# Transposing x tiles in pairs by column half, moving three small loads to GpSimd's queue, and dropping two filler products, at the head of a gated attention/MLP kernel

## The chip, the cores and the metric

The kernel runs on one core of one Trainium2 chip. The metric is device time in microseconds (us) of one execution.

The engines are TensorE (PE in the profile; PEld is its weight load), VectorE (DVE), ScalarE (ACT), GpSimd (POOL) and SyncE (SP). SPq, ACTq and POOLq in the profile are those engines issuing data transfers. "L592" is line 592 of the kernel in question; the changed kernel's lines are numbered 9 lower from the transposes on, because its text is shorter.

## The reference, cut to what matters

```
x: [1, 2048, 512] bf16
g   = sigmoid((x * gate_w).sum(-1))
qkv = x @ wqkv                        # 32 heads of 16, as [3, heads, S, 16]
o   = for each position: softmax over 8 keys at distance 0, 2, ..., 14, times their values
a   = o @ wo
h   = layernorm(x)
b   = token-mixing MLP over S: gelu(h^T @ w1 + b1) @ w2 + b2, transposed back
out = g * a + (1 - g) * b
```

Q, K and V come from x with its 512 columns on the partitions, so x has to be transposed. The first 512 rows (four tiles, x0 to x3) are transposed by TensorE. The other 1536 rows are transposed by three DMA transposes that SyncE issues.

## The kernel before: the parts that matter

The kernel builds a list of operations with their dependences. A list scheduler with estimated durations then fixes each engine's order before anything runs. TensorE's order is the order of the source, except for two operations (`sum0`, `sum1`).

```python
# loads; "sp" is SyncE's queue, "act" is ScalarE's
for k_ in (0, 2):
    xq(k_, "sp");  xq(k_ + 1, "act")      # x tiles, 128 KB each
    wqq(k_, "sp"); wqq(k_ + 1, "act")     # rows of wq, 128 KB each
load("gw", ...); load("b1", ...); load("b2", ...)     # 1, 3.5 and 4 KB, on SyncE
load("wk", ...)                                        # 512 KB
ld_w("wv", 2, 0, 4, "wv")                              # 512 KB
for k_ in range(1, 4):
    ld_x(4 * k_, 4)                                    # four x tiles
    ld_xt(k_)                                          # DMA transpose of 512 rows of x

# head of TensorE's program
pe_tx(0)                  # four 128x128 transposes of tile 0, into two banks
pe_tx(1)
PE(f_fill(2), ...)        # two products of ones, results unused
pe_q0(0, 0)               # Q of rows 0-255,   wq row block 0: 4 products of 256 columns
pe_tx(2)
pe_tx(3)
pe_q0(0, 1)
PE(f_tb, ...)             # b1, gate_w, b2 turned onto partitions
pe_q0(1, 0); pe_q0(1, 1)  # Q of rows 256-511, wq row blocks 0 and 1
pe_q0(2, 2); pe_q0(2, 3)  # all 512 rows, wq row blocks 2 and 3
# ... then K of rows 0-511 (first operation that needs wk), V, and the rest

# of each transposed tile, VectorE copies columns 0-255 and ScalarE columns 256-511
def xt_ev(t):
    for k_, eng in enumerate(("dve", "act")):
        ...

# VectorE: layernorm statistics of each x tile; attention products of 128x4096 each.
# After the second of these products GpSimd issues a transfer of 1 MB, SBUF to SBUF,
# that adds one buffer to another:
def qaddd(x_, y_, s_, h=h):
    o_, i_ = (sub(PB[b_], s_ * 4096, [(1, 4096)]) for b_ in (x_, y_))
    qkd[h, s_] = sch.dma("pool", lambda e: e.dma_start(o_, i_, accum_op=ALU.add, ...), ...,
                         reads=[PS[y_][s_]], writes=[PS[x_][s_]], ...)
```

Of the kernel before, what the change touches and what calls it, by code (L numbers as in the profile page):

```python
# [5 lines left out]
BF16 = mybir.dt.bfloat16  # L6
# [3 lines left out]
AF = mybir.ActivationFunctionType  # L10
AX = mybir.AxisListType

S = 2048
# [5 lines left out]
NST = S // 128  # L19
NFT = F // 128  # L20
# [260 lines left out]
class _Mem:  # L281
# [17 lines left out]
    def view(self, name, dtype, dims, extra=0, p0=0, np_=128):  # L299
        base = self.arena[:].bitcast(dtype)  # L300
        pst = base.ap[0][0]
        esz = mybir.dt.size(dtype)
        o = self.off[name]
        assert o % esz == 0
        return bass.AP(base.tensor, p0 * pst + o // esz + extra, [[pst, np_]] + [list(d) for d in dims])


def bass_gated_mix__sliding_local_dilated__mixer_token_mlp__prompt_kernel(nc, A_x, A_wqkv, A_wo, B_x, B_w1, B_b1, B_w2, B_b2, gate_w, out, dbg=None):
    with contextlib.ExitStack() as es:
# [37 lines left out]
        ps = es.enter_context(nc.psum_tensor("ps", [128, 8, 512], FP32))  # L347
        esem = {e: es.enter_context(nc.semaphore("sem_" + e)) for e in ("pool", "act", "dve", "pe")}
        sch = _Sched()
        A = sch.add  # L350
# [8 lines left out]
        X = view("X", BF16, [(D, NST), (1, D)])  # L359
        XT = view("XT", BF16, [(S, 4), (1, S)])  # L360
# [39 lines left out]
        IDENT = view("IDENT", BF16, [(1, 128)])  # L400
        ONES = view("ONES", BF16, [(1, 128)])
        RP = view("RP", BF16, [(1, 32)])
        GWREP = view("GWREP", BF16, [(32, 4), (1, 32)])
        MASK = view("MASK", BF16, [(PAD, NW), (1, PAD)], np_=32)
        B1R = view("ROWS", BF16, [(1, 128)], np_=NFT)
        B2R = view("ROWS", BF16, [(1, 128)], extra=128, np_=NST)
        GWR = view("ROWS", BF16, [(1, 128)], extra=256, np_=4)
        so = [0]

        def small(n, dims=None, extra=0):  # L410
            v_ = view("SMALL", FP32, dims or [(1, n)], extra=so[0] + extra)
            so[0] += n
            return v_
# [17 lines left out]
        B1C = small(NFT)  # L431
        B2C = small(NST)
# [5 lines left out]
        def psb(bank):  # L438
            return ps[:, bank, :].bitcast(BF16)

        def sub(ap_, offs, dims):
            return bass.AP(ap_.tensor, ap_.offset + offs, [list(ap_.ap[0])] + [list(d) for d in dims])
# [8 lines left out]
        def act(o_, i_, f_, **kw):  # L451
            return lambda e: e.activation(out=o_, in_=i_, func=f_, **kw)  # L452
# [32 lines left out]
        def load(name, dst, src, nbytes, writes, transpose=False, queue="sp", issue=0.5, order=True, deps=(), after=()):  # L485
            ds = sch.dsem(name)

            def fn(e):
                if transpose:
                    return e.dma_start_transpose(dst, src)  # L490
                return e.dma_start(dst, src)  # L491
            op = sch.dma(queue, fn, nbytes, ds, issue=issue, writes=writes, deps=list(deps) + late_dep[0],
                         after=list(after) + ([last_ld[queue]] if order and queue in last_ld else []), name=name)
            if order:
                last_ld[queue] = op
            return op
# [4 lines left out]
        def ld_w(name, tn, d0, d1, res):  # L501
            load(name, WQKV[:, d0:d1, tn * D:(tn + 1) * D], wqkv_v[:, d0:d1, tn * D:(tn + 1) * D], (d1 - d0) * 128 * D * 2, [res])
# [14 lines left out]
        for k_ in (0, 2):  # L517
# [1 line left out]
            xq(k_ + 1, "act")  # L519
            wqq(k_, "sp")  # L520
            wqq(k_ + 1, "act")
        load("gw", GWR, gate_w.rearrange("(t p) -> t p", p=128), 1024, ["gwr"], issue=0.4)
        load("b1", B1R, B_b1.rearrange("(t p) -> t p", p=128), 4096, ["b1r"], issue=0.4)
        load("b2", B2R, B_b2.rearrange("(t p) -> t p", p=128), 4096, ["b2r"], issue=0.4)
        load("wk", WQKV[:, 0:4, D:2 * D], wqkv_v[:, 0:4, D:2 * D], 4 * 128 * D * 2, ["wk"])
        ld_w("wv", 2, 0, 4, "wv")
        for k_ in range(1, 4):
            ld_x(4 * k_, 4)
# [12 lines left out]
        C1 = nc.const_aps.tensor(1.0, (128, 128), BF16)  # L541
# [9 lines left out]
        def PE(fn, dur, reads, writes, name, prio=0):  # L551
            op = A("pe", fn, dur, reads=reads, writes=writes, after=([chain[0]] if chain[0] is not None else []), name=name, prio=prio)
            chain[0] = op
            return op

        PE(f_warm, 2.6, [], ["b7"], "warm")

        def f_fill(n):
            def fn(e):
                ins = None  # L560
                for _ in range(n):
                    ins = e.matmul(ps[:, 0, 0:256], lhsT=C1, rhs=nc.const_aps.tensor(1.0, (128, 256), BF16), start=True, stop=True)
                return ins
            return fn

        def f_tx(t):
            def fn(e):
                ins = None
                for dt in range(4):
                    o_ = (dt % 2) * 128  # L570
                    ins = e.transpose(out=psb(4 + 2 * (t % 2) + dt // 2)[:, o_:o_ + 128],  # L571
                                      in_=X[:, t, dt * 128:(dt + 1) * 128], identity=IDENT)
                return ins
            return fn

        extl = {}

        def xt_ev(t):
            for k_, eng in enumerate(("dve", "act")):
                bk = 4 + 2 * (t % 2) + k_  # L580
                src = sub(psb(bk), 0, [(128, 2), (1, 128)])
                dst = sub(XT, 2 * k_ * S + t * 128, [(S, 2), (1, 128)])
                extl[eng] = A(eng, (lambda s_, d_: lambda e: e.tensor_copy(out=d_, in_=s_))(src, dst) if eng == "dve" else act(dst, src, AF.Copy),  # L583
                  0.27 if eng == "dve" else 0.35, reads=["b%d" % bk], writes=["xt0_%d_%d" % (t, k_)], name="ext%d_%d" % (t, k_), prio=-30)

        def f_q0(hb, dt):
            c0, c1 = ((0, 256), (256, 512), (0, 512))[hb]
# [7 lines left out]
            return fn  # L595

        def pe_tx(t):
            PE(f_tx(t), 0.35, ["x%d" % t, "ident"], ["b%d" % (4 + 2 * (t % 2)), "b%d" % (5 + 2 * (t % 2))], "tx%d" % t)
            xt_ev(t)

        def pe_q0(hb, dt):
            PE(f_q0(hb, dt), 0.87 if hb == 2 else 0.44, ["xt0_%d_%d" % (t_, dt // 2) for t_ in ((0, 1), (2, 3), (0, 1, 2, 3))[hb]] + ["wq%d" % dt], ["b%d" % dl for dl in range(4)],
               "q0_%d_%d" % (hb, dt))

        def f_tb(e):
            e.transpose(out=psb(4)[:, 512:512 + NFT], in_=B1R, identity=IDENT[0:NFT, 0:NFT])  # L606
            e.transpose(out=psb(4)[:, 576:580], in_=GWR, identity=IDENT[0:4, 0:4])  # L607
            return e.transpose(out=psb(4)[:, 544:544 + NST], in_=B2R, identity=IDENT[0:NST, 0:NST])  # L608

        pe_tx(0)  # L610
        pe_tx(1)
        PE(f_fill(2), 0.4, [], ["b0"], "fill1")
        pe_q0(0, 0)
        pe_tx(2)
        pe_tx(3)
        pe_q0(0, 1)
        PE(f_tb, 0.17, ["b1r", "b2r", "gwr", "ident"], ["b4"], "t_b12")
        A("dve", lambda e: e.tensor_copy(out=GWREP, in_=sub(psb(4), 576, [(1, 4), (0, 32)])), 0.2, reads=["b4"], writes=["gwrep"], name="gwrep", prio=-20)
        A("dve", lambda e: e.tensor_copy(out=B1C, in_=psb(4)[:, 512:512 + NFT]), 0.15, reads=["b4"], writes=["b1c"], name="b1c", prio=-20)
        A("dve", lambda e: e.tensor_copy(out=B2C, in_=psb(4)[:, 544:544 + NST]), 0.15, reads=["b4"], writes=["b2c"], name="b2c", prio=-20)  # L620
        pe_q0(1, 0)
        pe_q0(1, 1)
        pe_q0(2, 2)
        pe_q0(2, 3)
        XT0 = ["xt0_%d_%d" % (t, k_) for t in range(4) for k_ in range(2)]

# [48 lines left out]
        for dl in range(4):  # L675
# [3 lines left out]
          reads=["k%d_1" % dl for dl in range(4)], writes=["khalo"], name="khalo")  # L679
# [10 lines left out]
        for t in range(NST):  # L690
            A("dve", (lambda t_: lambda e: e.bn_stats(out=ST6[:, t_, :], in_=X[:, t_, :]))(t), 0.67,  # L691
              reads=["x%d" % t], writes=["st%d" % t], name="st%d" % t, prio=-20, after=[extl["dve"]])
# [6 lines left out]
          reads=["md"], writes=["vv"], name="ln_var", prio=-20)  # L699
# [3 lines left out]
          reads=["ms", "rstd"], writes=["nmr"], name="ln_nmr", prio=-20)  # L703
        for t in range(NST):
            A("dve", (lambda t_: lambda e: e.tensor_scalar(out=X[:, t_, :], in0=X[:, t_, :], scalar1=col(RSTD, t_), scalar2=col(NMR, t_),  # L705
                                                           op0=ALU.mult, op1=ALU.add))(t), 0.33,
              reads=["rstd", "nmr", "st%d" % t], writes=["x%d" % t], name="ln%d" % t, prio=-10)
# [22 lines left out]
        for h in range(2):  # L730
# [27 lines left out]
            for s_ in range(2):  # L758
                qadd(bb[0], bb[2], s_)
            b0 = bb[0]  # L760
            A("pe", f_sum(h, b0, h == 0), 1.2 + (1.0 if h == 0 else 0), reads=PS[b0] + ["rp"] + ((XTALL + ["gwrep"]) if h == 0 else []),
              writes=LGB + (["b3"] if h == 0 else []), name="sum%d" % h, prio=-100, delay=0.2)
# [4 lines left out]
            if h == 0:  # L767
                A("dve", tt(psub(LOG[0], 0, 32, 0, [(UT_, NW), (1, PAD)]), psub(LOG[0], 0, 32, 0, [(UT_, NW), (1, PAD)]), MASK, ALU.add), 0.2,
                  reads=["mask"], writes=["log0"], name="msk", prio=-30)
# [16 lines left out]
            for c in range(4):  # L786
                src = psub(ATT[h], 32 * c, 32, 0, [(0, 4), (1, NW * UT_)])
                dst = sub(AVW[h], c * NW * UT_, [(1, NW * UT_)])
                prev = sch.dma("pool", (lambda d_, s_: lambda e: e.dma_start(d_, s_))(dst, src), 524288, sch.dsem("av%d_%d" % (h, c)), issue=1.0,  # L789
                               reads=["att%d" % h], writes=["avw%d_%d" % (h, c)] + al, after=[prev] if prev else [], name="av%d_%d" % (h, c))  # L790
# [11 lines left out]
          reads=["ebt"], writes=["e1"], name="e1", prio=-20)  # L802
# [60 lines left out]
        for ft in range(NFT):  # L863
            bank = MLPB[ft]
            for half in range(2):
# [3 lines left out]
              reads=["b%d" % bank, "b1c"], writes=["ut%d" % ft] + (["wq0", "wq1", "wq2", "wq3", "wk", "wv"] if ft == 0 else []), name="gel%d" % ft, table=GELU)  # L869
# [56 lines left out]
        for hf, (c0, c1) in enumerate(CH):  # L926
            bank = lastb[hf]
            PE(f_wo(L, bank, c0, c1), 0.44, ["ot%d" % (L // 2), "wo"], ["b%d" % bank], "wo%d_%d" % (L, hf))
            if hf == 0:
                A("act", act(OUTS[:, 4, c0:c1], ps[:, bank, 0:c1 - c0], AF.Identity, scale=col(OMG, L), bias=col(C2, L)), 0.55,  # L930
                  reads=["b%d" % bank, "omg", "c2"], writes=["outs4"], name="ev%da" % L)
            else:
                A("dve", (lambda bank_, a_, b_: lambda e: e.tensor_scalar(out=OUTS[:, 4, a_:b_], in0=ps[:, bank_, 0:b_ - a_], scalar1=col(OMG, L),  # L933
                                                                          scalar2=col(C2, L), op0=ALU.mult, op1=ALU.add))(bank, c0, c1), 0.35,
                  reads=["b%d" % bank, "omg", "c2"], writes=["outs4h"], name="ev%db" % L)
# [82 lines left out]
```

## Time and profile before

Before: 165.93 us (median of 3; 165.66 to 166.41). The profiled execution took 165.79 us.

| what | value |
|---|---|
| span of the profiled execution | 164.1 us |
| TensorE / VectorE busy | 97% / 92% |
| first x transpose on TensorE | 3.73 us |
| first Q product / first K product | 5.12 / 9.73 us |
| wk issued / landed | 3.85 / 9.60 us |
| x2, x3, wq2 landed | 5.19, 5.38, 5.94 us |

The page's part 1 (busy time, share of the span, number of instructions) and the first line of its part 4 (share of the chain that ended last, by engine), kernel before:

```profile
PE 159.4 (97%) x792; PEld 77.0 (47%) x808; DVE 150.7 (92%) x126; ACT 75.4 (46%) x104; POOL 11.9 (7%) x35
...
PE 93%; DMA 2%; SPq 1%; ACT 1%; issue 1%
```

TensorE bounds the kernel: almost all of the chain is TensorE work. The timeline of TensorE in the head of the kernel before (start us, length us, engine, line, operation, shapes, count, and in brackets idle time and what ended it):

```profile
3.73 1.01 PE L571 MATMUL ps<-arena 128*128 128x128 bf16 x8 [0.16 <-DMA arena<-in_A_x_dram]
4.53 0.57 PE L562 MATMUL ps<-const-bfloat16-1.0 128*128 128x256 bf16 x2
5.12 0.63 PE L592 MATMUL ps<-arena 128*128 128x256 bf16 x4
5.59 0.61 PE L571 MATMUL ps<-arena 128*128 128x128 bf16 x8
6.04 0.60 PE L592 MATMUL ps<-arena 128*128 128x256 bf16 x4
6.78 0.16 PE L606 MATMUL ps<-arena 14*128 14x14 bf16 x1
...
6.92 2.79 PE L592 MATMUL ps<-arena 128*128 128x256 bf16 x15
9.73 1.46 PE L659 MATMUL ps<-arena 128*128 128x512 bf16 x6
```

Eight transposes, two fillers, four Q products, eight transposes, four Q products, the bias transposes, the rest of Q, and K from 9.73 us. From there TensorE never waits, so the time of this kernel is the start of K plus a constant.

The timeline of VectorE, kernel before:

```profile
11.43 2.29 DVE L449 TENSOR_TENSOR arena<-arena 128x4096 bf16<-128x4096 bf16 x1 [0.39 <-ACT arena L452]
13.64 2.46 DVE L691 BATCH_NORM_STATS2 arena<-arena 128x6 f32<-128x512 bf16 x4
16.67 2.47 DVE L691 BATCH_NORM_STATS2 arena<-arena 128x6 f32<-128x512 bf16 x4 [0.56 <-DMA arena<-in_A_x_dram]
19.06 2.27 DVE L449 TENSOR_TENSOR arena<-arena 128x4096 bf16<-128x4096 bf16 x1
```

The second 128x4096 product runs at 19.06 us, behind the statistics of x8 to x11. GpSimd's accumulating transfer is issued after it, as the timeline of GpSimd shows:

```profile
21.64 1.32 POOL L746 DMA_DIRECT2D arena<-arena  x1 [19.56 <-DVE arena L449]
```

### The profile page before, as it was taken

Reading aid. Unit: us, or ns where it says so; the run is one execution under the profiler, and the core shown is the slowest. Engines: PE = TensorE matmul, PEld = TensorE weight load, DVE = VectorE, ACT = ScalarE, POOL = GpSimd, SP = SyncE. Lnnn points to the kernel's source line nnn. Section 1 sums busy time; section 2 is a strip of 40 time slices with the busy share of each in tenths; the row PEclk is TensorE's granted clock in tenths of the full one; section 3 lists DMA queues with packets and bytes.
Section 4 is the critical chain, followed back from the end, with each engine's and each line's share of the span. In section 5 each row is a group of like instructions: output and inputs, shape, how many; then the busy total and the mean of one; then the engine's idle time right before and its main releaser. Section 6 shows DMA issues by size and latency. Waiting matters only on the chain.

```text
span 164.1 us, 1991 instructions
## 1 busy us (share of the span) xinstructions
PE 159.4 (97%) x792; PEld 77.0 (47%) x808; DVE 150.7 (92%) x126; ACT 75.4 (46%) x104; POOL 11.9 (7%) x35
## 2 busy tenths in 40 slices
PE   7999999999999999999999999999999999999993
PEld 3745555555544444444444344444444444444641
DVE  0679999999999999999999999999999999999950
ACT  3356677666773699953211669210121111111164
POOL 3000030020000000005000000005000222000000
PEclk9999999999999999999999999999999999999999
DMA  4999999919499287999998994993996899981014
GB/s 153 284 240 249 258 178 252 185 22 188 92 310 290 50 230 202 291 290 259 158 205 245 278 250 145 295 242 113 280 226 177 164 205 184 211 201 36 32 57 135
DMA packets 44668, 32.24 MB, mean 197 GB/s; under 512 B 7924, under 2 KB 42228, under 8 KB 44660
## 3 DMA queue, kind: packets, MB, share of 16 engines
q1 hardware_dynamic: 41428, 22.06, 51.8%
q0 software_dynamic: 2512, 9.44, 28.9%
q10 hardware_dynamic: 720, 0.62, 1.1%
q8 instruction: 6, 0.10, 0.2%
q14 instruction: 2, 0.02, 0.0%
HBM read 18.88 MB, written 2.10 MB: 128 GB/s over the span
## 4 chain that ended last, share of the span: by engine, by line
PE 93%; DMA 2%; SPq 1%; ACT 1%; issue 1%
PE ps L857 29%; PE ps L884 29%; PE ps L659 23%; PE ps L893 8%; DMA arena<-in_B_b_dram 2%; PE ps L592 2%; SPq L491 1%; PE ps L721 1%; ACT arena L452 1%; PE ps L716 1%; PE ps L606 0%; PE ps L608 0%; PE ps L607 0%
## 5 line engine op out<-in xcount | busy, mean ns | idle before, releaser
L449 DVE TENSOR_TENSOR arena<-arena 128x4096 bf16<-128x4096 bf16 (+8 forms) x79 | 131.9, 1718 | 1.3 <-ACT arena L452 0.4
L884 PE MATMUL ps<-arena 128*128 128x512 bf16 (+2 forms) x234 | 50.0, 366 | 0.2
L857 PE MATMUL ps<-arena 128*128 128x512 bf16 x218 | 48.5, 379 | 0.3
L452 ACT ACTIVATE arena<-ps,arena 128x512 bf16<-128x512 f32 (+1 forms) x30 | 21.8, 732 | 58.0 <-PE ps L893 40.5
L452 ACT ACTIVATE arena<-ps 128x512 bf16<-128x512 f32 (+3 forms) x53 | 33.1, 629 | 18.4 <-PE ps L659 10.9
L659 PE MATMUL ps<-arena 128*128 128x512 bf16 x173 | 38.0, 379 | 0.2
L884 PEld LDWEIGHTS ps<-arena 128*128 128x128 bf16 x238 | 22.8, 98 | 25.9
L857 PEld LDWEIGHTS ps<-arena 128*128 128x128 bf16 x224 | 21.7, 98 | 26.9 <-ACT arena L452 0.7
L659 PEld LDWEIGHTS ps<-arena 128*128 128x128 bf16 x176 | 19.8, 113 | 18.3 <-DVE arena L691 0.5
L893 PE MATMUL ps<-arena 128*128 128x512 bf16 (+2 forms) x66 | 15.5, 366 | 0.1
L953 ACT ACT_TABLE_LOAD x11 | 14.1, 1283 | 2.9 <-issue 2.7
L691 DVE BATCH_NORM_STATS2 arena<-arena 128x6 f32<-128x512 bf16 x16 | 10.0, 679 | 0.7 <-DMA arena<-in_A_x_dram 0.6
L452 ACT ACTIVATE arena<-arena 128x16 f32<-128x16 f32 (+5 forms) x10 | 6.8, 679 | 7.3 <-DVE arena L449 7.0
L893 PEld LDWEIGHTS ps<-arena 128*128 128x128 bf16 x68 | 6.5, 98 | 7.3
L789 POOL DMA_DIRECT2D arena<-arena x8 | 4.3, 561 | 73.9 <-DVE arena L449 73.9
L705 DVE TENSOR_SCALAR arena<-arena 128x512 bf16<-128x512 bf16 x16 | 5.3, 402 | 0.0
L826 POOL DMA_DIRECT2D arena<-arena x3 | 3.6, 1210 | 18.9 <-DVE arena L449 18.9
L746 POOL DMA_DIRECT2D arena<-arena x2 | 2.5, 1268 | 31.4 <-DVE arena L449 31.4
L583 DVE COPY arena<-ps 128x256 bf16<-128x256 bf16 x4 | 1.1, 292 | 3.7 <-PE ps L571 3.6
L592 PE MATMUL ps<-arena 128*128 128x256 bf16 (+1 forms) x23 | 4.0, 307 | 0.1
L933 DVE TENSOR_SCALAR arena<-ps,arena 128x128 bf16<-128x128 f32 x1 | 0.4, 408 | 3.5 <-PE ps L893 3.5
L546 PE MATMUL ps<-const-bfloat16-1.0 128*128 128x512 bf16 (+1 forms) x9 | 2.7, 486 | 0.9 <-PEq L1003 0.9
(35 smaller groups left out, 17.5 us busy)
## 6 DMA issues: line engine op xcount, KB each, us to landing
arena<-in_B_w_dram SPq DMA_DIRECT2D x7, 1024.0 KB, 7.6
arena<-in_B_w_dram SPq DMA_DIRECT2D x8, 896.0 KB, 8.5
arena<-arena POOLq DMA_DIRECT2D x5, 1024.0 KB, 9.8
arena<-arena POOLq DMA_DIRECT2D x8, 512.0 KB, 11.1
out_dram<-arena SPq DMA_DIRECT2D x15, 128.0 KB, 1.7
arena<-in_A_x_dram SPq DMA_DIRECT2D x3, 512.0 KB, 4.9
arena<-in_A_wqkv_dram SPq DMA_DIRECT2D x2, 512.0 KB, 6.2
arena<-in_A_wo_dram SPq DMA_DIRECT2D x1, 512.0 KB, 8.3
```

Of the source, the lines that this page charges most:

```text
L449: return lambda e: e.tensor_tensor(out=o_, in0=a_, in1=b_, op=op_)
L452: return lambda e: e.activation(out=o_, in_=i_, func=f_, **kw)
L592: ins = e.matmul(ps[:, dl, c0:c1], lhsT=sub(WQKV, dt * 3 * D + dl, [(4, 128)]), rhs=XT[:, dt, c0:c1], start=(dt == 0 and hb == 0), stop=(d ...
L659: ins = e.matmul(ps[:, bank, :], lhsT=sub(WQKV, dt * 3 * D + tn * D + dl, [(4, 128)]), rhs=XT[:, dt, sb * 512:(sb + 1) * 512], start=(dt = ...
L691: A("dve", (lambda t_: lambda e: e.bn_stats(out=ST6[:, t_, :], in_=X[:, t_, :]))(t), 0.67, reads=["x%d" % t], writes=["st%d" % t], name="s ...
L705: A("dve", (lambda t_: lambda e: e.tensor_scalar(out=X[:, t_, :], in0=X[:, t_, :], scalar1=col(RSTD, t_), scalar2=col(NMR, t_), op0=ALU.mu ...
L789: prev = sch.dma("pool", (lambda d_, s_: lambda e: e.dma_start(d_, s_))(dst, src), 524288, sch.dsem("av%d_%d" % (h, c)), issue=1.0, reads= ...
L826: sch.dma("pool", (lambda o_, i_: lambda e: e.dma_start(o_, i_, accum_op=ALU.add, max_dma_last_dim=4096))(pw(0, 4), pw(4, 4)), 1800000, sc ...
L857: ins = e.matmul(ps[:, bank, :], lhsT=W1H[ft // 2][:, st, 128 * (ft % 2):128 * (ft % 2) + 128], rhs=X[:, st, :], start=(st == 0), stop=(st ...
L884: ins = e.matmul(ps[:, bank, 0:c1 - c0], lhsT=W2S[i // 2][:, ft, 128 * (i % 2):128 * (i % 2) + 128], rhs=UT[:, ft, c0:c1], start=(ft == 0) ...
L893: ins = e.matmul(ps[:, bank, 0:c1 - c0], lhsT=OT[:, i // 2, dl, 128 * (i % 2):128 * (i % 2) + 128], rhs=WO[:, dl, c0:c1], start=False, sto ...
L953: e.preload_act_table_set(want)
```

## The change

Its intent is to let Q start earlier and keep TensorE from waiting in the head. The three small loads leave SyncE's queue, so that wk is issued earlier. The x tiles are transposed two at a time, one column half after the other. One tile of a pair is copied by VectorE, the other by ScalarE, so the first half is ready sooner. The fillers go, and the bias transposes move behind the Q products.

```diff
-        load("gw", ..., issue=0.4)
-        load("b1", ..., issue=0.4)
-        load("b2", ..., issue=0.4)
         load("wk", ...)
+        load("gw", ..., issue=0.6, queue="pool")
+        load("b1", ..., issue=0.6, queue="pool")
+        load("b2", ..., issue=0.6, queue="pool")
...
-        def f_fill(n): ...
-        def f_tx(t):                 # four transposes of tile t
+        def f_tx(t, k_):             # two transposes: column half k_ of tile t
...
-        def xt_ev(t):
-            for k_, eng in enumerate(("dve", "act")):
+        def xt_ev(t, k_):
+            eng = ("dve", "act")[t % 2]
...
         def pe_tx(t):
-            PE(f_tx(t), 0.35, ...)
-            xt_ev(t)
+            for k_ in range(2):
+                for t_ in (t, t + 1):
+                    PE(f_tx(t_, k_), 0.2, ...)
+                    xt_ev(t_, k_)
...
         pe_tx(0)
-        pe_tx(1)
-        PE(f_fill(2), 0.4, [], ["b0"], "fill1")
         pe_q0(0, 0)
+        pe_q0(0, 1)
         pe_tx(2)
-        pe_tx(3)
-        pe_q0(0, 1)
-        PE(f_tb, 0.17, ..., ["b4"], "t_b12")    # and its three copies
+        pe_q0(0, 2)
         pe_q0(1, 0)
         pe_q0(1, 1)
-        pe_q0(2, 2)
+        pe_q0(1, 2)
+        PE(f_tb, 0.17, ..., ["b7"], "t_b12")    # and its three copies
         pe_q0(2, 3)
```

More of the change, by code (lines that the diff above doesn't have):

```diff
@@ L521, in bass_gated_mix__sliding_local_dilated__mixer_token_mlp__prompt_kernel @@
             wqq(k_ + 1, "act")
-        load("gw", GWR, gate_w.rearrange("(t p) -> t p", p=128), 1024, ["gwr"], issue=0.4)
-        load("b1", B1R, B_b1.rearrange("(t p) -> t p", p=128), 4096, ["b1r"], issue=0.4)
-        load("b2", B2R, B_b2.rearrange("(t p) -> t p", p=128), 4096, ["b2r"], issue=0.4)
         load("wk", WQKV[:, 0:4, D:2 * D], wqkv_v[:, 0:4, D:2 * D], 4 * 128 * D * 2, ["wk"])
+        load("gw", GWR, gate_w.rearrange("(t p) -> t p", p=128), 1024, ["gwr"], issue=0.6, queue="pool")
+        load("b1", B1R, B_b1.rearrange("(t p) -> t p", p=128), 4096, ["b1r"], issue=0.6, queue="pool")
+        load("b2", B2R, B_b2.rearrange("(t p) -> t p", p=128), 4096, ["b2r"], issue=0.6, queue="pool")
         ld_w("wv", 2, 0, 4, "wv")
@@ L556, in bass_gated_mix__sliding_local_dilated__mixer_token_mlp__prompt_kernel @@
         PE(f_warm, 2.6, [], ["b7"], "warm")
-        def f_fill(n):
+        def f_tx(t, k_):
             def fn(e):
                 ins = None
-                for _ in range(n):
-                    ins = e.matmul(ps[:, 0, 0:256], lhsT=C1, rhs=nc.const_aps.tensor(1.0, (128, 256), BF16), start=True, stop=True)
-                return ins
-            return fn
-        def f_tx(t):
-            def fn(e):
-                ins = None
-                for dt in range(4):
-                    o_ = (dt % 2) * 128
-                    ins = e.transpose(out=psb(4 + 2 * (t % 2) + dt // 2)[:, o_:o_ + 128],
-                                      in_=X[:, t, dt * 128:(dt + 1) * 128], identity=IDENT)
+                for d_ in range(2):
+                    ins = e.transpose(out=psb(4 + 2 * (t % 2) + k_)[:, d_ * 128:d_ * 128 + 128],
+                                      in_=X[:, t, (2 * k_ + d_) * 128:(2 * k_ + d_ + 1) * 128], identity=IDENT)
                 return ins
@@ L576, in bass_gated_mix__sliding_local_dilated__mixer_token_mlp__prompt_kernel @@
         extl = {}
-        def xt_ev(t):
-            for k_, eng in enumerate(("dve", "act")):
-                bk = 4 + 2 * (t % 2) + k_
-                src = sub(psb(bk), 0, [(128, 2), (1, 128)])
-                dst = sub(XT, 2 * k_ * S + t * 128, [(S, 2), (1, 128)])
-                extl[eng] = A(eng, (lambda s_, d_: lambda e: e.tensor_copy(out=d_, in_=s_))(src, dst) if eng == "dve" else act(dst, src, AF.Copy),
-                  0.27 if eng == "dve" else 0.35, reads=["b%d" % bk], writes=["xt0_%d_%d" % (t, k_)], name="ext%d_%d" % (t, k_), prio=-30)
+        def xt_ev(t, k_):
+            eng = ("dve", "act")[t % 2]
+            bk = 4 + 2 * (t % 2) + k_
+            src = sub(psb(bk), 0, [(128, 2), (1, 128)])
+            dst = sub(XT, 2 * k_ * S + t * 128, [(S, 2), (1, 128)])
+            extl[eng] = A(eng, (lambda e: e.tensor_copy(out=dst, in_=src)) if eng == "dve" else act(dst, src, AF.Copy),
+                          0.27 if eng == "dve" else 0.35, reads=["b%d" % bk], writes=["xt0_%d_%d" % (t, k_)], name="ext%d_%d" % (t, k_), prio=-30)
         def f_q0(hb, dt):
@@ L597, in pe_tx @@
         def pe_tx(t):
-            PE(f_tx(t), 0.35, ["x%d" % t, "ident"], ["b%d" % (4 + 2 * (t % 2)), "b%d" % (5 + 2 * (t % 2))], "tx%d" % t)
-            xt_ev(t)
+            for k_ in range(2):
+                for t_ in (t, t + 1):
+                    PE(f_tx(t_, k_), 0.2, ["x%d" % t_, "ident"], ["b%d" % (4 + 2 * (t_ % 2) + k_)], "tx%d_%d" % (t_, k_))
+                    xt_ev(t_, k_)
         def pe_q0(hb, dt):
@@ L605, in f_tb @@
         def f_tb(e):
-            e.transpose(out=psb(4)[:, 512:512 + NFT], in_=B1R, identity=IDENT[0:NFT, 0:NFT])
-            e.transpose(out=psb(4)[:, 576:580], in_=GWR, identity=IDENT[0:4, 0:4])
-            return e.transpose(out=psb(4)[:, 544:544 + NST], in_=B2R, identity=IDENT[0:NST, 0:NST])
+            e.transpose(out=psb(7)[:, 512:512 + NFT], in_=B1R, identity=IDENT[0:NFT, 0:NFT])
+            e.transpose(out=psb(7)[:, 576:580], in_=GWR, identity=IDENT[0:4, 0:4])
+            return e.transpose(out=psb(7)[:, 544:544 + NST], in_=B2R, identity=IDENT[0:NST, 0:NST])
         pe_tx(0)
-        pe_tx(1)
-        PE(f_fill(2), 0.4, [], ["b0"], "fill1")
         pe_q0(0, 0)
+        pe_q0(0, 1)
         pe_tx(2)
-        pe_tx(3)
-        pe_q0(0, 1)
-        PE(f_tb, 0.17, ["b1r", "b2r", "gwr", "ident"], ["b4"], "t_b12")
-        A("dve", lambda e: e.tensor_copy(out=GWREP, in_=sub(psb(4), 576, [(1, 4), (0, 32)])), 0.2, reads=["b4"], writes=["gwrep"], name="gwrep", prio=-20)
-        A("dve", lambda e: e.tensor_copy(out=B1C, in_=psb(4)[:, 512:512 + NFT]), 0.15, reads=["b4"], writes=["b1c"], name="b1c", prio=-20)
-        A("dve", lambda e: e.tensor_copy(out=B2C, in_=psb(4)[:, 544:544 + NST]), 0.15, reads=["b4"], writes=["b2c"], name="b2c", prio=-20)
+        pe_q0(0, 2)
         pe_q0(1, 0)
         pe_q0(1, 1)
-        pe_q0(2, 2)
+        pe_q0(1, 2)
+        PE(f_tb, 0.17, ["b1r", "b2r", "gwr", "ident"], ["b7"], "t_b12")
+        A("dve", lambda e: e.tensor_copy(out=GWREP, in_=sub(psb(7), 576, [(1, 4), (0, 32)])), 0.2, reads=["b7"], writes=["gwrep"], name="gwrep", prio=-20)
+        A("dve", lambda e: e.tensor_copy(out=B1C, in_=psb(7)[:, 512:512 + NFT]), 0.15, reads=["b7"], writes=["b1c"], name="b1c", prio=-20)
+        A("dve", lambda e: e.tensor_copy(out=B2C, in_=psb(7)[:, 544:544 + NST]), 0.15, reads=["b7"], writes=["b2c"], name="b2c", prio=-20)
         pe_q0(2, 3)
```

## The prediction

> **What bounds the kernel.** TensorE. The chain of waits gives it 93% of a 164.1 us span, and it runs without a gap from 6.78 us to the end. Before that the chain is: SyncE's queue issues eight small loads one after the other (0.75 to 3.4 us), the last of them b2; b2 lands at 6.64; the bias transposes (L606) start at 6.78. VectorE is busy 92% but ends its attention work at 158.05 us, 1.7 us before wo14 needs it. So only time won before the first K projection (L659, 9.73 us) counts, and at most about 1.3 us can be won there: from the first x transpose (3.73 us) TensorE needs 16 transposes and 16 x 512 columns of Q products, about 4.7 us, and takes 6.0.
>
> **Where those 6.0 us go** (timeline, first 12 us). (a) Q's first product waits to 5.12 because VectorE copies tile 0 and tile 1 one after the other (4.35 to 5.07) and the copies of tile 1 can only start after its four transposes. The filler hides that wait (4.53 to 4.96). (b) 0.14 us of gap before L606, waiting for b2. (c) 0.18 us before L659: wk was issued at 3.85, behind the three small loads, and landed at 9.60. The loads themselves leave a hole in the DMA: from 5.5 to 6.1 us hardly anything moves, against 360 GB/s around it.
>
> **What the change does.**
> - Pairing: tile 0 goes to VectorE and tile 1 to ScalarE, one copy each per half. The first Q product then waits for ScalarE's first copy (start 4.34, 0.385 us): start about 4.78 instead of 5.12, -0.34.
> - Filler gone (2 x 0.213 us at half clock); a real gap of about 0.25 us stands at 4.53.
> - Reordered Q products have two more 256-column groups in place of one 512 group: cost within 0.05 us.
> - Bias transposes go last but one, at about 7.9 us, with b2 coming over GpSimd. No wait there: -0.2 to -0.3.
> - SyncE issues wk about 1.18 us earlier (2.67). [...]I expect it landed at about 8.4 to 8.8 and not waited for: -0.18. The later loads and x transposes move up alike.
>
> Adding the Q stage up with the trace's times (0.109 us per 256 columns, 0.056 per transpose, 0.216 per 512), Q ends at about 8.9 and K starts there: 0.8 us earlier. VectorE's first attention product then starts about 1 us earlier (11.43 to 10.4), so the later meetings of the two engines (first logits sum at 53.06, last wo) keep their slack and the 0.8 us reach the end.
>
> **Predicted: 165.1 us (164.6 to 165.7).** Faster by over 2%: 0.01; within 2%: 0.98; slower by over 2%: 0.01.
>
> **What would show it.** First Q product at 4.7 to 4.9; no gap before the bias transposes; wk landed before 8.9; first K product at 8.8 to 9.1; gapless TensorE afterwards; first 128x4096 VectorE product near 10.4.
>
> **What would make it wrong.** (1) wk lands later than 9: the gain falls to 0.3 to 0.6. (2) The clock: the profile goes from half to full at 4.91 us. [...] (3) GpSimd's loads are slow: [...] Later than 7.9, TensorE and VectorE would wait.

The sum came to 0.8 us, 165.93 to 165.1, with -0.18 for wk, whose landing at 8.4 to 8.8 is the estimate from the 9.60 and the 1.18 us of earlier issue that the profile of before gives.

## More of the kernel before

VectorE's and ScalarE's orders are whatever the scheduler makes of the estimates.

## The result

| | median us | range | executions |
|---|---|---|---|
| before | 166.06 | 165.64 to 166.41 | 6 |
| after | 165.87 | 165.57 to 166.28 | 6 |

The ratio is 0.9991, with a 95% interval of 0.9968 to 1.0014: no difference. (Here and below, a ratio is the mean time of one kernel's executions over that of the other's in the same rounds, so it is not quite the ratio of the medians quoted.) I had forecast 165.1, at most 165.7. In the tables below, medians and ranges are of all executions of a run, those included.

The page's same two lines, kernel after. The chain is now TensorE through and through: it no longer waits for b2, and it is no faster.

```profile
PE 160.6 (98%) x810; PEld 77.6 (47%) x810; DVE 150.7 (92%) x126; ACT 75.4 (46%) x104; POOL 13.7 (8%) x38
...
PE 97%; ACT 1%; DVE 0%; issue 0%
```

The timeline of TensorE in the head, kernel after:

```profile
3.53 1.01 PE L562 MATMUL ps<-arena 128*128 128x128 bf16 x8
4.68 1.87 PE L583 MATMUL ps<-arena 128*128 128x256 bf16 x8
6.34 0.71 PE L562 MATMUL ps<-arena 128*128 128x128 bf16 x8
6.89 1.98 PE L583 MATMUL ps<-arena 128*128 128x256 bf16 x16
8.80 0.18 PE L599 MATMUL ps<-arena 14*128 14x14 bf16 x1
...
8.96 1.05 PE L583 MATMUL ps<-arena 128*128 128x512 bf16 x4
9.85 1.46 PE L650 MATMUL ps<-arena 128*128 128x512 bf16 x6
```

The first Q product starts at 4.68 us (forecast 4.7 to 4.9), 0.44 earlier than before. wk landed at 8.50 (forecast 8.4 to 8.8). But the first eight Q products took 1.66 us from 4.68 to 6.34, 0.21 each, where I had counted 0.11: TensorE was still at half clock. In the profile of before, the clock had gone to full at 4.91 us, and the spacing of equal products with it, from 0.213 to 0.109 us (128x128 transposes: 0.107 to 0.056); here, where the trace has no record of the clock, the spacing changes near 6.5. Also x2, x3 and wq2 landed at 5.91, 6.25 and 6.56 us, 0.6 to 0.9 later than in the profile of before. K starts at 9.85, not at 8.9.

The timelines of VectorE and GpSimd further on, kernel after, show what else moved:

```profile
11.66 2.29 DVE L449 TENSOR_TENSOR arena<-arena 128x4096 bf16<-128x4096 bf16 x1 [0.32 <-ACT arena L452]
13.87 2.46 DVE L682 BATCH_NORM_STATS2 arena<-arena 128x6 f32<-128x512 bf16 x4
16.25 2.27 DVE L449 TENSOR_TENSOR arena<-arena 128x4096 bf16<-128x4096 bf16 x1
18.45 4.83 DVE L682 BATCH_NORM_STATS2 arena<-arena 128x6 f32<-128x512 bf16 x8
```

```profile
18.83 1.28 POOL L737 DMA_DIRECT2D arena<-arena  x1 [14.80 <-DVE arena L449]
```

The second 128x4096 product has gone from 19.06 to 16.25 us, and with it the issue of GpSimd's 1 MB transfer from 21.64 to 18.83 us. In this execution nothing came of that. It matters below.

### The profile page after: what moved, and what is told of

Its sections match the earlier page's. It is cut to its first block, busy times and chain, and to the rows that moved or that the text cites. A ratio compares the mean times of both kernels' runs of the same rounds, so it can differ in the third digit from the quotient of the medians.

```text
span 164.2 us, 2008 instructions
## 1 busy us (share of the span) xinstructions
PE 160.6 (98%) x810; PEld 77.6 (47%) x810; DVE 150.7 (92%) x126; ACT 75.4 (46%) x104; POOL 13.7 (8%) x38
## 4 chain that ended last, share of the span: by engine, by line
PE 97%; ACT 1%; DVE 0%; issue 0%
PE ps L848 30%; PE ps L875 29%; PE ps L650 23%; PE ps L884 8%; PE ps L583 3%; PE ps L546 2%; PE ps L712 1%; ACT arena L452 1%; PE ps L562 1%; PE ps L707 1%; DVE arena L574 0%; PE ps L599 0%; PE ps L601 0%; PE ps L600 0%
## 5 line engine op out<-in xcount | busy, mean ns | idle before, releaser
L875 PEld LDWEIGHTS ps<-arena 128*128 128x128 bf16 x238 | 22.8, 98 | 25.9
L848 PEld LDWEIGHTS ps<-arena 128*128 128x128 bf16 x224 | 21.7, 98 | 26.9 <-ACT arena L452 0.7
L650 PEld LDWEIGHTS ps<-arena 128*128 128x128 bf16 x176 | 19.9, 113 | 18.1
L884 PEld LDWEIGHTS ps<-arena 128*128 128x128 bf16 x68 | 6.5, 98 | 7.3
L583 PE MATMUL ps<-arena 128*128 128x256 bf16 (+1 forms) x28 | 4.9, 328 | 0.1
L583 PEld LDWEIGHTS ps<-arena 128*128 128x128 bf16 x28 | 3.0, 121 | 1.1 <-DVE arena L574 0.4
```

Of the source, the lines that this page charges most:

```text
L583: ins = e.matmul(ps[:, dl, c0:c1], lhsT=sub(WQKV, dt * 3 * D + dl, [(4, 128)]), rhs=XT[:, dt, c0:c1], start=(dt == 0 and hb == 0), stop=(d ...
L650: ins = e.matmul(ps[:, bank, :], lhsT=sub(WQKV, dt * 3 * D + tn * D + dl, [(4, 128)]), rhs=XT[:, dt, sb * 512:(sb + 1) * 512], start=(dt = ...
L848: ins = e.matmul(ps[:, bank, :], lhsT=W1H[ft // 2][:, st, 128 * (ft % 2):128 * (ft % 2) + 128], rhs=X[:, st, :], start=(st == 0), stop=(st ...
L875: ins = e.matmul(ps[:, bank, 0:c1 - c0], lhsT=W2S[i // 2][:, ft, 128 * (i % 2):128 * (i % 2) + 128], rhs=UT[:, ft, c0:c1], start=(ft == 0) ...
L884: ins = e.matmul(ps[:, bank, 0:c1 - c0], lhsT=OT[:, i // 2, dl, 128 * (i % 2):128 * (i % 2) + 128], rhs=WO[:, dl, c0:c1], start=False, sto ...
```

## The experiments

All 18 runs gave correct results. "K" is the start of the first K product in the profiled execution.

### First round: is it the filler, the loads, or chance?

Three theories for the missing 0.8 us. "Gap": without the filler, TensorE's clock rises later. "Chance": the moment of the rise is not tied to the program. "Contention": the early wk and GpSimd's loads delay x2, x3 and wq2. Four kernels separate them.

**b_again**: the kernel before, unchanged.

> The kernel before, unchanged, for a second profile. Theory 'chance': [...] (it was 4.91 in the first profile of before and about 6.5 in that of the changed kernel). Theory 'gap': the gap left by the filler moved it, so here, with the filler, it is again at 4.9 us within 0.2. Both: x2 and x3 land at 5.2 and 5.4 us, within 0.2.

**loads_only**: before, with only the loads moved.

```diff
-        load("gw"/"b1"/"b2", ..., issue=0.4)      # ahead of wk, on SyncE
         load("wk", ...)
+        load("gw"/"b1"/"b2", ..., issue=0.6, queue="pool")
```

> Only the three small loads moved to GpSimd (and with that wk issued 1.18 us earlier); TensorE's order and the filler as before. Theory 'contention': these loads and the early wk take DMA time from the x and wq tiles: x2, x3, wq2 land at about 5.9, 6.2, 6.5 us instead of 5.2, 5.4, 5.9, and K starts no earlier than 9.4 although wk lands at 8.5. Rival, 'late x was chance': x2 and x3 land at 5.2 and 5.4, b2 no longer holds TensorE, K starts at about 9.4 with an early clock. Theory 'gap': the clock doubles at 4.9, as the filler is there.

**pairs_only**: the changed kernel with that edit undone.

> The changed kernel with the small loads back on SyncE ahead of wk. Theory 'contention': x2, x3, wq2 land at 5.2, 5.4, 5.9 again; wk at 9.6, and then K starts no earlier than 9.7, so nothing is won over before (165.9 to 166.1 us). Theory 'gap': the clock doubles at 6.5 here too. Theory 'chance': it doubles anywhere.

**after_fill**: the changed kernel with one filler product back.

```diff
         pe_tx(0)
+        PE(f_fill(1), 0.2, [], ["b0"], "fill1")
         pe_q0(0, 0)
```

> The changed kernel with one filler product of 256 columns back in the gap before the first Q product. Theory 'gap': the clock doubles at 4.9 again, the first eight Q products take 0.11 us each instead of 0.21, and the time falls by 0.2 to 0.8 us below the changed kernel's 165.87. Theory 'chance': the doubling is not tied to it; the mean time stays within 0.2 us of the changed kernel's. Theory 'contention': x3 lands at 6.2 and TensorE waits for it wherever the clock doubled early.

| run | median us (range) | ratio to before, 95% | full clock at | x3, wq2 landed | K |
|---|---|---|---|---|---|
| b_again | 166.28 (166.03 to 166.42) | 1.0011 (0.9991 to 1.0031) | about 6.6 | 5.85, 6.30 | 9.98 |
| loads_only | 166.63 (166.41 to 167.28) | 1.0045 (1.0019 to 1.0070) | 4.92 | 5.84, 6.83 | 10.30 |
| pairs_only | 167.72 (165.76 to 168.35) | 1.0041 (0.9992 to 1.0090) | about 5.8 | 6.29, 6.74 | 9.71 |
| after_fill | 166.28 (165.43 to 166.74) | 1.0001 (0.9972 to 1.0030) | 4.08 | 5.88, 6.71 | 9.68 |

- "Gap" falls. The kernel before, with its fillers, got its full clock at 6.6 us in one execution and at 4.91 in another. Pairs_only, without filler, got it at 5.8.
- The first profile of before happened to show early tiles. Already its repeat had x3 and wq2 0.4 to 0.5 us later.
- Even with an early clock (after_fill, 4.08) K was at 9.68. TensorE then waited 0.2 us for x3 and 0.5 us for wq2. (It also stood still for 0.4 us near 24 us; the reason comes in the third round.)
- Loads alone are a loss: b2 landed at 7.39 us over GpSimd's queue (6.64 over SyncE's in the first profile), and the bias transposes, early in this order, waited for it (7.53 instead of 6.78).
- Pairs_only had an unexpected group: four of its six executions took 167.7 to 168.4 (two of these are over 1.5% above the fastest; the granted clock was 1.0 in all four). I first put this down to a late full clock in the runs without filler; the texts below call this theory "missed window".

### Second round: what is the slow group?

**a_again**: the changed kernel, unchanged.

> The changed kernel, unchanged, for a second profile and five more times. Theory 'chance' ([...]seen so far 4.08, 4.91, 4.92, 5.75, 6.45, 6.6): another value, and mean times within 0.3 us of before's. Theory 'late tiles': x3 lands near 6.2 and wq2 near 6.7 whatever the clock, and the first K product comes 2.9 to 3.1 us after the later of wq2 and the second transposes, at 9.6 to 9.9. Theory 'missed window' (pairs_only had four executions near 168 us): without filler some executions of this kernel too take 167.5 or more.

**b_nofill**: before, without its fillers.

```diff
-        PE(f_fill(2), 0.4, [], ["b0"], "fill1")
```

> The kernel before without its two filler products and nothing else. TensorE then stands still from 4.4 to 5.0 us. Theory 'missed window': some of the six executions [...]take 167.5 us or more, the others 165.4 to 166.4 as before. Theory 'chance': no such group, all within 165.4 to 166.5.

**pairs_fill**: pairs_only plus the one filler of after_fill.

> Pairs_only with one filler product of 256 columns behind the first transposes. Theory 'missed window': the group near 168 us is gone, all six take 165.3 to 166.5. Rival, 'slow for another reason': some of the six are again near 168.

**late_small**: a candidate. It is after_fill with the small loads moved to the end of SyncE's x loads, the bias transposes moved into bank 3 about 30 us later, and the second half of Q reordered:

```diff
         pe_tx(2)
-        pe_q0(0, 2)
         pe_q0(1, 0)
         pe_q0(1, 1)
-        pe_q0(1, 2)
+        pe_q0(2, 2)
```

> A version meant to be better: pairs kept, one filler kept, small loads on SyncE behind all x tiles, bias transposes 30 us later in a bank that is free, and the second column half of Q takes wq0 and wq1 before wq2 is asked for. Theory 'late tiles': wq2 is now needed near 7.7 and no longer waited for; K starts at 8.9 to 9.5 depending on the clock, and the time is 165.2 to 165.6, 0.4 to 0.8 below before. Rival, 'the loads of wk hold K': K starts when wk lands, 8.5 to 9.6, and the gain stays under 0.4.

| run | median us (range) | ratio to before, 95% | full clock at | x3, wq2 landed | K |
|---|---|---|---|---|---|
| a_again | 166.29 (165.77 to 167.65) | 1.0019 (0.9985 to 1.0053) | 3.86 | 6.19, 6.69 | 9.67 |
| b_nofill | 166.06 (165.81 to 166.43) | 0.9994 (0.9971 to 1.0017) | 3.75 | 6.00, 6.48 | 10.04 |
| pairs_fill | 167.18 (165.82 to 168.63) | 1.0023 (0.9983 to 1.0063) | about 6.2 | 5.62, 5.88 | 9.74 |
| late_small | 166.42 (166.16 to 167.55) | 1.0027 (0.9998 to 1.0056) | 5.14 | 6.41, 6.93 | 9.91 |

"Missed window" falls on both sides: b_nofill has a real gap and no slow group, and pairs_fill has its filler and has one. Late_small is no better either; with its order TensorE waited 0.5 us behind the second transposes for VectorE's copies of them. wq2, at 6.93, had landed before it was asked for, so the expectation held on that point, but K did not come earlier.

By luck the profiled execution of a_again was a long one, 167.65 us. Its K started early, at 9.67. The timeline of TensorE, a_again, around 24 us:

```profile
21.75 2.75 PE L650 MATMUL ps<-arena 128*128 128x512 bf16 x12
26.23 2.11 PE L650 MATMUL ps<-arena 128*128 128x512 bf16 x9 [1.73 <-DMA arena<-in_A_x_dram]
```

TensorE stands still for 1.73 us (about 1.9 between products) until a transfer from x has landed. The chain of waits of a_again up to there (start us, length us, what):

```profile
16.64 0.04 issue
16.69 9.41 DMA arena<-in_A_x_dram
26.10 0.14 issue
26.23 3.83 PE ps L650 x17
```

The transfer is the last of the three DMA transposes of x. It was issued at 16.69 us and landed 9.41 us later. In the profile of before the same transpose was issued at 17.16 and landed 6.0 us later, at 23.16. Between the two lies GpSimd's accumulating transfer, issued at 18.64 instead of 21.64.

The first lines of a_again's own Q stage also show how the tiles hold it when the clock is early (timeline of TensorE, a_again):

```profile
4.68 1.04 PE L583 MATMUL ps<-arena 128*128 128x256 bf16 x8 [0.34 <-DVE arena L574]
6.03 0.72 PE L562 MATMUL ps<-arena 128*128 128x128 bf16 x8 [0.30 <-DMA arena<-in_A_x_dram]
6.74 1.94 PE L583 MATMUL ps<-arena 128*128 128x256 bf16 x16
```

The eight Q products are issued in 0.88 us now, but the second transposes have to wait for x2 and x3 and the next Q products for wq2. By the starts of single instructions in the trace these waits add up to 0.7 us. That is as much as the late clock cost in the first profile of after (8 products times 0.104 us, 0.8 us). One or the other takes the gain.

### Third round: the collision, tested from both sides

New theory, "collision": VectorE's new order issues GpSimd's transfer 2.8 us earlier, onto the last x transpose, which in some executions then lands late and holds TensorE near 24 us.

**a_hold**: the changed kernel, where GpSimd's transfer must wait for that transpose. All engines keep the changed kernel's order.

```diff
     def qaddd(x_, y_, s_, h=h):
...
-                                     issue=1.3, reads=[PS[y_][s_]], ...
+                                     issue=1.3, reads=[PS[y_][s_], "xt3"], ...
```

> The changed kernel with one dependence more: GpSimd's first accumulating 1 MB transfer is not issued before the last x transpose has landed. Every engine's order is the changed kernel's. Theory 'collision' (VectorE's new order issues that transfer at 18.7 instead of 21.5 us, on top of the last x transpose, which then lands up to 3.4 us late and holds TensorE near 24 us): the transpose lands within 6.1 us of its issue, no stall near 24 us, no execution over 166.5, median 165.6 to 166.0. Rival, 'slow for another reason': some executions of the six still over 166.8.

**b_early**: the kernel before, with VectorE's second 128x4096 product moved to where the changed kernel has it, and nothing else.

```diff
         est = sch.schedule()
+        o_ = sch.order["dve"]
+        mv = [op for op in o_ if op.name == "qk0_1_0"][0]
+        o_.remove(mv)
+        o_.insert([op.name for op in o_].index("st7") + 1, mv)
```

> The kernel before, where VectorE does its second 128x4096 product ahead of the statistics of x8 to x11, as the changed kernel does; nothing else is moved. Theory 'collision': GpSimd's transfer is issued near 18.8 instead of 21.5, the last x transpose (issued near 16.5 to 17.2) lands 7 to 9.5 us after its issue instead of 6.0, TensorE stalls 0.5 to 2.5 us near 24 us, and most executions take 166.5 to 168.5. Rival, 'collision is harmless': transpose after 6.0 us, times 165.4 to 166.5 as before.

**pairs_fill_hold**: pairs_fill plus the edit of a_hold.

> The candidate for best: pairs, one filler, small loads on SyncE as before, and the accumulating transfer held behind the last x transpose. Theory 'collision': the executions of 167.6 to 168.6 that pairs_fill showed are gone; all within 165.3 to 166.4, median near 165.8, 0.2 to 0.4 below before. Rival, 'slow for another reason': again some above 167.5.

**wk_held**: a_hold, with wk not issued before wq2 has landed.

```diff
         est = sch.schedule()
+        by = {op.name: op for op in sch.ops}
+        by["wk"].deps.add(by["wq2"])
```

> a_hold with wk not issued before wq2 has landed. Theory 'wk crowds the tiles': without wk behind it wq2 lands at 5.8 to 6.3 instead of 6.6 to 6.8, TensorE's Q stage is 0.3 to 0.5 us shorter where the clock was early, but wk now lands at 9.3 or later and sets K's start at 9.4 or later. Rival, 'arrivals are chance': wq2 lands anywhere from 5.9 to 6.9 as in the other profiles.

| run | median us (range) | ratio to before, 95% | last transpose: issue to landing | GpSimd's transfer issued |
|---|---|---|---|---|
| a_hold | 165.82 (165.16 to 166.34) | 0.9979 (0.9951 to 1.0007) | 6.00 | 22.13 |
| b_early | 166.47 (165.65 to 170.00) | 1.0025 (0.9979 to 1.0070) | 9.40 | 18.09 |
| pairs_fill_hold | 165.57 (165.13 to 165.66) | 0.9965 (0.9945 to 0.9986) | 5.91 | 23.11 |
| wk_held | 166.73 (166.24 to 167.01) | 1.0038 (1.0016 to 1.0060) | 5.96 | 24.04 |

The timeline of TensorE, b_early, shows the stall, put into the kernel before by moving one VectorE instruction:

```profile
21.84 2.11 PE L659 MATMUL ps<-arena 128*128 128x512 bf16 x9
25.47 2.75 PE L659 MATMUL ps<-arena 128*128 128x512 bf16 x12 [1.53 <-DMA arena<-in_A_x_dram]
```

The same stretch of a_hold runs through:

```profile
21.78 6.42 PE L650 MATMUL ps<-arena 128*128 128x512 bf16 x29
```

The collision is shown from both sides: adding it to the kernel before makes a slow group (the profiled execution took 166.86, and others 168.1 and 170.0, neither of them traced), and taking it away from the two kernels that had it removes it. a_hold's six executions would prove little alone, because only 3 of 18 of the changed kernel went over 166.6. The weight lies on the traces and on pairs_fill (four of six over 166.6) against its held twin (none of twelve, with best_again below). It does not strike each time. I had expected most executions of b_early to suffer; three of six stayed within 165.65 to 166.07.

The trace says more about its nature. In all profiles where GpSimd's transfer was issued early, its first packet appears about 0.1 us before the last data packets of the transpose, and those start 5.4 to 5.5 us after the issue, as in the other kernels before and a_hold. In a_again the last data packet starts at 22.10 us and the landing is reported at 26.10. So the data of the transpose is not moved later; it is its completion that comes late. The view of DMA queues, a_again, from 22.2 to 24.8 us and then from 24.8 to 25.8 us (queue, packets, MB, share of 16 engines; q0 is GpSimd's queue and q1 SyncE's):

```profile
q0 software_dynamic: 143, 0.59, 112.8%
...
q0 software_dynamic: 48, 0.20, 98.2%
q1 hardware_dynamic: 32, 0.00, 4.4%
```

For 2.6 us only GpSimd's packets start. Then 32 packets of 4 bytes start on SyncE's queue, between 24.90 and 25.71 us, and the 16 completion updates of the transpose follow, 25.57 to 26.10. In the profile of after, which was not harmed, the same 32 packets start at 21.20 to 21.36 us, with the last data. So it is the start of the small packets behind the data that is held back. What holds these packets back, no run here shows, so the mechanism stays open.

The early transfer left the transpose unharmed in three profiles (after, pairs_fill, late_small: 5.94 to 6.01 us from issue to landing) and delayed it in five (6.98 to 9.41, against 5.53 to 6.01 in the other fifteen of all 20). The time between the two issues tells them apart:

| profile | transpose's issue to GpSimd's issue | transpose's issue to landing |
|---|---|---|
| late_small / pairs_fill / after | 3.27 / 3.12 / 2.94 | 5.94 / 6.01 / 5.99 |
| pairs_only | 2.68 | 6.98 |
| after_fill | 2.42 | 8.39 |
| a_third / b_early / a_again | 2.23 / 2.16 / 1.96 | 9.37 / 9.40 / 9.41 |

The closer the two issues, the longer the delay. These eight profiles were sorted after the fact; no run was made to test the limit.

wk_held is a loss as a kernel, because wk now lands at 10.09, but it shows what the Q stage is worth with on-time tiles. In the timeline of TensorE, wk_held:

```profile
8.16 1.05 PE L583 MATMUL ps<-arena 128*128 128x512 bf16 x4
10.13 1.05 PE L650 MATMUL ps<-arena 128*128 128x512 bf16 x4 [0.92 <-DMA arena<-in_A_wqkv_dram]
```

With the full clock at 4.17 us and x3 and wq2 landed at 5.54 and 6.09, the last Q product was issued by 8.83, so Q was through at about 9.05. That is the 8.9 of my sum, to 0.15. In this one profile the sum was right; its inputs were not typical. Good inputs help the old order too: in b_early, which has TensorE's order of before, the clock was full before 3.5 us, x3 and wq2 landed at 5.43 and 5.68, and K started at 9.10.

### Fourth round: why are the tiles late?

**wk_held2**: wk_held once more.

> The kernel of wk_held once more, for a second profile. Theory 'wk crowds the tiles': wq2 lands at 5.8 to 6.3 again. Theory 'GpSimd's loads crowd them' or 'chance': nothing keeps it from 6.5 to 6.9.

**loads_held** and **loads_held2**: a_hold, with GpSimd's small loads not issued before wq3 has landed.

```diff
         est = sch.schedule()
+        by = {op.name: op for op in sch.ops}
+        by["gw"].deps.add(by["wq3"])     # b1 and b2 follow on the same queue
```

> a_hold with GpSimd's three small loads not issued before wq3 has landed; wk stays right behind wq2. The bias transposes then wait for b2 and the time gets worse, which is not the question. Theory 'wk crowds the tiles': wq2 lands at 6.5 to 7.0 as in a_hold. Theory 'GpSimd's loads crowd them': wq2 lands at 5.7 to 6.3.

> The kernel of loads_held once more, for a second profile; the same expectations.

**pfh_wq1**: pairs_fill_hold, with wk not issued before wq1 has landed.

> pairs_fill_hold with wk not issued before wq1 has landed (near 4.4 instead of 3.85 us). Theory 'wk crowds the tiles': wq2 lands at 5.7 to 6.3, wk at 8.4 to 9.2, K starts at 9.0 to 9.5, and the median is 165.0 to 165.5. Rival, 'arrivals are chance': like pairs_fill_hold, 165.4 to 165.7. Either way no execution over 166.5.

| run | us | wq2 landed | wk landed |
|---|---|---|---|
| wk_held2 | 166.48 (one execution, state unknown) | 6.45 | 10.33 |
| loads_held | 173.07 (one execution, state unknown) | 6.50 | 8.94 |
| loads_held2 | 173.30 (one execution, state unknown) | 6.89 | 9.37 |
| pfh_wq1 | 166.28 (164.90 to 166.99) | 6.55 | 10.84 |

Both one-sided theories are weak. Without GpSimd's early loads wq2 is still late, so they are not needed for it. Without the early wk it landed at 6.09 once and at 6.45 and 6.55 in two other profiles, so wk is at most part of it. Over all 20 profiles, wq2 landed at 6.50 to 6.93 us, on average 6.74, in the nine where wk stands right behind it in SyncE's queue, and at 5.68 to 6.74, on average 6.31, in the other eleven. The early wk seems to cost wq2 about 0.4 us; the ranges overlap, and what scatters the rest stays open.

pfh_wq1 is not a better kernel: its ratio to before is 0.9986 (0.9959 to 1.0014). wk was issued a little later and landed as late as 10.84, so K started at 10.89 in the profile. Two of its six executions passed the 166.5 that I had called the limit; in the traced one, 166.99, the transpose landed after 5.94 us, so it was the late wk and not the collision.

loads_held shows by accident that the clock also falls. TensorE waited 5.7 us for b2, and the granted clock fell to 0.50 and rose again. The view of busy time by stretch, loads_held (after the length: PE, PEld, DVE, ACT, POOL busy us, then granted clock, DMA share, GB/s):

```profile
4.00:11.00 7.00, 4.04 (x37) 3.17 (x35) 2.85 (x7) 1.43 (x4) 2.55 (x19) 1.00 1.10 302
11.20:18.00 6.80, 3.47 (x11) 1.52 (x13) 2.34 (x6) 1.10 (x3) 0.00 (x0) 0.50 1.05 244
18.00:25.00 7.00, 7.00 (x34) 3.63 (x33) 6.39 (x6) 4.79 (x9) 0.00 (x0) 1.00 1.05 273
```

The records of the clock in the trace put its changes at 4.34, 11.17 and 18.00 us, 6.83 us apart both times; in loads_held2 at 4.28, 11.11 and 17.94, again 6.83 apart. What sets this spacing, no run here shows. In 20 profiles (five have no clock record; there I read the rise from the spacing of the products) the first rise came between before 3.5 us (b_early) and 6.80 us (a_third), a spread of more than 3 us, and late rises came with fillers (b_again, about 6.6) and without (a_third).

### Fifth round: what is left of the gain?

**best_again**: pairs_fill_hold once more. **a_third**: the changed kernel beside it.

> pairs_fill_hold once more. Theory 'the pairing is worth what is left of it': median 165.4 to 165.8, 0.2 to 0.5 below before's of the same rounds, no execution over 166.5. Rival, 'luck': within 0.15 of before.

> The changed kernel beside it. Theory 'collision': most executions at 165.5 to 166.3 and one or two of six above 166.6 or even 167; median 0.2 to 0.6 above best_again.

best_again: 165.81 us (165.18 to 166.48), ratio 0.9984 (0.9957 to 1.0012). a_third: 166.03 us (165.80 to 167.54), ratio 1.0013 (0.9981 to 1.0046). The profiled execution of a_third is the one of 167.54: its last transpose landed 9.37 us after its issue, and TensorE stalled as in a_again.

All executions together, each a mean over several chips and therefore only a rough comparison (wk_held and pfh_wq1, which hold the transfer too, are left out because their wk comes late):

| kernels | executions | mean us | highest | over 166.6 |
|---|---|---|---|---|
| before | 62 | 166.11 | 166.70 | 1 |
| after | 18 | 166.22 | 167.65 | 3 |
| with the transfer held (a_hold, pairs_fill_hold, best_again) | 18 | 165.69 | 166.48 | 0 |

With the collision taken away, the pairing is worth an estimated 0.4 us, the difference of these means. The last row mixes two kernels: pairs_fill_hold also keeps a filler and SyncE's small loads. The change itself with the transfer held is a_hold alone, mean 165.74, and its interval (0.9951 to 1.0007) includes no gain. The changed kernel's mean is 0.5 above the held row's. Its three executions over 166.6 make 0.2 of that; the other 15 average 165.99, and what makes the rest is not traced. pairs_fill_hold measured 0.35% and 0.16% below before in two sets of rounds. The second set's interval includes no gain, and either is far under 2%.

## Why the prediction was wrong, point by point

- **Right: TensorE bounds the kernel, and only time won before K counts.** Time minus the start of K is 156.05 to 156.11 us in thirteen unstalled profiles of ten kernels.
- **Right: the single steps of the loads and the pairing.** The first Q product started at 4.68 us (forecast about 4.78), wk landed at 8.50 (8.4 to 8.8), and nothing in the head waited for b2, which landed at 7.14, 4.4 us after its issue at 2.72 (over SyncE's queue in the profile of before, 3.2). That was later than I had allowed.
- **Wrong: "Adding the Q stage up with the trace's times [...], Q ends at about 8.9 and K starts there: 0.8 us earlier".** This step failed in its inputs. I took the moment of the full clock (4.91 us) and the landings of x2, x3 and wq2 (5.19, 5.38, 5.94) from one profile, as if they belonged to the kernel. The baseline was a quick sample too: a median of 165.93 us from three executions, against a mean of 166.11 over 62. They vary between executions: the clock from under 3.5 to 6.8 us, wq2 from 5.68 to 6.93. The new order leans on wq2 more than the old: it asks for it right behind the second transposes, near 6.2 us, where the old order asked for it at 7.82. That it leans more on the clock is not shown. So a late clock (after: 0.8 us) or late tiles (a_again: 0.7 us) eat the gain. Where both were good, in wk_held, Q ended within 0.15 us of my figure. Over many executions, and with the transfer held, about half of the forecast was there: 166.11 to 165.69, 0.4 us.
- **Wrong: "the later meetings of the two engines [...] keep their slack and the 0.8 us reach the end".** VectorE's first attention product did not move to 10.4 us but started at 11.66 (11.43 before), and the change of VectorE's order issued a 1 MB transfer 2.8 us earlier. In some executions that holds the completion of the last x transpose by up to 3.4 us, and TensorE with it by up to 1.9. The three long executions of 18 raise the changed kernel's mean by 0.2 us; the whole distance to the held kernels is 0.5. I had looked for what the engines wait on, and not for what a moved instruction sets off on the DMA queues.
- **The clock was on my list of dangers, for the wrong reason.** I feared that the gap left by the filler would make the clock rise late; how, and what it would cost, was not shown. In b_nofill, without filler, the clock rose at 3.75 us and no execution was slow; in b_again, with fillers, it rose at 6.6. So the filler does not decide it.
- **In the first six executions of after** no collision was bad (highest 166.28), so there the lost Q gain is enough to explain the result: 0.9991, about 0.15 us. One of the six was traced, with no stall after K; the other five were not.

## What to carry to other kernels

A stage at the very start of a kernel should be forecast from several profiles, because clock and first landings can differ between executions by as much as the change may win: here the clock rose between under 3.5 and 6.80 us, and wq2, 128 KB issued at 2.2 us, landed between 5.68 and 6.93. When a change moves work on an engine that is off the critical path, ask which transfers that work releases and what they meet: here one VectorE instruction, moved 2.8 us forward, held TensorE for up to 1.9 us in some executions, more than the 0.4 that the transposes gained on average. And look at the spread of the executions, not only at their median: a group 2 us above the rest was the first sign.
